# A two-layer FFN chain behind attention on one core: state products of two column pairs in one group inside a projection

## The chip, the cores and the metric

The kernel runs on 1 core of one Trainium2 chip. The metric is the device time of one execution in microseconds (us), lower is better. Engines are called TensorE (PE in the profile; PEld is its weight load), VectorE (DVE), ScalarE (ACT), GpSimd (POOL) and SyncE (SP, the DMA queue).

## The reference

x is (8 token blocks, 8 heads, 512 tokens, 64), state is (8, 8, 32, 64). For each block and head the tokens read the states with softmax attention, and the states read the tokens:

```
scores = scale * x @ state^T ; a = softmax(scores) ; xread = a @ state
scores2 = scale * state @ x^T ; a2 = softmax(scores2) ; sread = a2 @ x
rows = concat([xread, sread])          # 8 * 544 = 4352 rows of 512
y = (silu(rows @ w_gate) * (rows @ w_val)) @ w_out        # inner width 1536
h = y @ w_in2 ; out = (max(h,0) + alpha*min(h,0)) @ w_out2 # inner width 2048
```

## The kernel before

The rows of xread are never formed. Since xread = a @ state, the first FFN's gate and value for a token block are a @ (state @ w). So for each block b and each pair of 128-wide columns j (NJ1 = 6 pairs, of gate and of value together 512 columns) the kernel forms the **state products** state @ w, 128 rows (4 heads of 32 states) by 512 columns, one for each of two units g (`StateTimesW`, L566 to 592). A unit issues four products, one for each head, each a stationary tile of 64 rows by 32 columns and 512 moving columns. Unit g = 0 lies on rows 0 to 63 of the array, g = 1 on rows 64 to 127, and its four heads on the four groups of 32 columns. In float32 each is two matmul instructions, so a pair (b, j) has 16. The result stands in a PSUM bank. `hi` (L584, ScalarE, printed as the helper's L122) copies it as float32r, and `lo` (L588, VectorE, helper L128) subtracts that from it. Both parts go to an SBUF tile `sw` and are the stationary operands of gate and value.

All large products are done as three float32r passes over high and low parts (`PASSES`, L19): high by high, high by low, low by high.

`ffn1` (L702) goes through the 12 column tiles f of a block, here called **iterations**: the gate's 6 matmuls into PSUM bank `g` and Silu on ScalarE (`silu`, L648); the value's 6 into bank `v` and a multiplication on VectorE (`times`, L655); `split` into a high part (ScalarE, L663) and a low part (VectorE, L667); and the projection of the *previous* tile, 3 matmuls into each of four accumulators e = 0 to 3 (`project`, L678). In iteration 0 the projection is the last one of the block before, whose four accumulators are then copied out (`give`, L697). Between these, `fill(f, 0)` runs after the gate, `fill(f, 1)` after the split, and `fill(f, 2)` after the projection, from a table of slots. Gate(f) uses the state products of pair f // 2.

The slots of a block (`ffn1_slots`, L749) hold: the state products of pair j in slot (2j - 2, 2), that is behind the projection of iteration 2j - 2 and one iteration ahead of gate(2j); those of the next block's pair 0 in slot (10, 2); `paced` steps of the second FFN's weight preparation in iterations 1, 2, 5, 6, 9, 10 (two ScalarE, two VectorE and one GpSimd instruction, and further ones from a list, `one_later`); and the next block's attention, for its two halves of the heads g = 0 and 1 in iterations 2, 3, 5, 6, 6 and 6, 7, 9, 10, 10 (L782). Its loads stand in iterations 0 and 4 (L780). Attention's scores (L241), turned sums (L314) and state reads (L325) use TensorE for short groups, always into the two PSUM banks of the tag `aux`.

PSUM has eight banks: four accumulators, `g`, `v` and two `aux`. Before the change the state products use the two `aux` banks, one for each unit. The `sw` tiles come from 16 tiles of the tag `t4`, which the hidden tiles h, the raw x tiles and the prepared weights of the second FFN share.

The order on TensorE is the order in which the code issues (`manual_schedule` for PE, L724). The order on ScalarE, VectorE, GpSimd and SP is set by a planner that takes ready work by program order in its own model of time; each engine then works its list strictly in that order. The start (blocks 0 and 1) has an order of all engines written out by hand (L25). `ffn1` runs for blocks 2 to 7 (XT = 2, L933). Behind them come a small block of 256 state rows and the second FFN, which are not touched.

Of the kernel before, what the change touches and what calls it, by code (L numbers as in the profile page):

```python
# [70 lines left out]
def attention_and_two_ffns(ctx: ExitStack, tc: tile.TileContext, x, state, w_gate, w_val,  # L71
                           w_out1, w_in2, w_out2, alpha, out):
    nc = tc.nc
    B, H, S, D = x.shape
# [4 lines left out]
    P = 128  # L79
    T = S + Ns  # L80
    NPAIR = H // 2
    NG = H // 4
    NF1, NF2 = F1 // P, F2 // P
    NJ1, NJ2 = NF1 // 2, NF2 // 2
# [4 lines left out]
    XT = 2  # L89
# [12 lines left out]
    def name(s):  # L102
        uid[0] += 1
        return f"{s}_{uid[0]}"

    def t8(shape, dt, s):
        return p8.tile(shape, dt, tag="t8", name=name(s))

    def t4(shape, dt, s):
        return p4.tile(shape, dt, tag="t4", name=name(s))  # L110

    def t2(shape, dt, s):
        return p2.tile(shape, dt, tag="t2", name=name(s))

    def psum(shape, tag, bufs=1):
        return ps.tile(shape, F32, tag=tag, name=name(tag), bufs=bufs)

    def aux(shape):
        return psum(shape, "aux", 2)
# [28 lines left out]
    stt, xq, xn, wraw, wo1, sw, a1, srs = {}, {}, {}, {}, {}, {}, {}, []  # L148
# [49 lines left out]
    def load_xq(b, g, jj):  # L198
        t = t2([P, S // 32, 32], F32, "xq")
        for hp in range(2):  # L200
            for e in range(2):
                q = 64 * hp + 32 * e
                nc.sync.dma_start(
                    t[q:q + 32],
                    x[b, 4 * jj + 2 * hp + g].rearrange("(t i) d -> i t d", i=32)[:, :, 32 * e:32 * e + 32])
        xq[b, g, jj] = t

    def load_xn(b, g, eng=nc.sync, n=1):
        src = x[b].rearrange("(h g) (p c) d -> g p h c d", g=NG, c=SC)[g]
        t = t4([P, 4, SC, D], F32, "xn")  # L210
        for i in reversed(range(n)):
            h = slice(4 // n * i, 4 // n * (i + 1))
            eng.dma_start(t[:, h].rearrange("p h c d -> p h (c d)"), src[:, h].rearrange("p h c d -> p h (c d)"))
        xn[b, g] = t.rearrange("p h c d -> p c h d")
# [335 lines left out]
    later = []  # L550
# [7 lines left out]
    for j in range(NJ2):  # L558
        for src, take in ((words(w_in2, 0, NPAIR, 2 * P * j, 2 * P * (j + 1)), take_w2(j)),
                          (words(w_out2, 2 * j, 2 * j + 2, 0, DM), take_wo2(j))):  # L560
            n = src.shape[1] // 2
# [4 lines left out]
    class StateTimesW:  # L566
        def __init__(self, b, j, g):
            self.b, self.j, self.g = b, j, g

        def product(self):  # L570
            b, j, g = self.b, self.j, self.g
            if b >= XT:
                sw.setdefault((b, j), []).append(t4([P, 2, 4 * P], F32R, "sw"))
            elif g == 0:
                t = t8([P, NG, 2, 4 * P], F32R, "sw")
                sw[b, j] = [t[:, g] for g in range(NG)]
            self.o = aux([P, 4 * P])
            q = slice(64 * g, 64 * g + 64)
            for c in range(NPAIR):
                nc.tensor.matmul(self.o[Ns * c:Ns * (c + 1), :], stt[b][q, 2 * c + g, :],  # L580
                                 wraw[j][q, c].rearrange("p k f -> p (k f)"), start=True, stop=True)
# [9 lines left out]
            self.hi()  # L591
            self.lo()

    def state_times_w(b, j):
        sw.pop((b, j), None)
        us = [StateTimesW(b, j, g) for g in range(NG)]
        for u in us:
            u.product()
        for u in us:
            u.parts()  # L600


    class Block:


        def __init__(self, n, lhs, rhs, nk, keep=False):
            self.n, self.lhs, self.rhs, self.nk, self.keep = n, lhs, rhs, nk, keep
            self.acc, self.p, self.hid = None, {}, {}
            self.banks = lambda f: ("g", "v")

        def product(self, f, which, tag):
# [66 lines left out]
        def project(self, f):  # L678
            if f == 0:
                self.start()  # L680
            for e in range(NPAIR):
                self.project_part(f, e)
            self.hid.pop(f)

# [39 lines left out]
    with tc.manual_schedule(engines={mybir.EngineType.PE}):  # L724
# [7 lines left out]
        def load_x(b, g):  # L732
            for jj in range(2):
                load_xq(b, g, jj)
            load_xn(b, g)

        def attention(b, at, later):

            for g in range(NG):
                u = att[b, g]  # L740
                for f, stage in zip(at, [[lambda u=u: u.xt(0), lambda u=u: u.xt(1)],
                                         [u.scores, u.first_cols, u.second_max, u.first_max, u.first_sub,
                                          u.second_exp, u.first_exp],
                                         [u.first_sum, u.first_eps, u.first_over, u.first_scale, u.second_sum, u.second_turn, u.second_copy],
                                         [u.second_read, u.second_times], [u.first_parts]]):
                    for th in stage:
                        yield f + later * g, th

        def ffn1_slots(b):  # L749
            slots = {}  # L750

            def put(f, i, th):
                slots.setdefault((f, i), []).append(th)

            def paced(th=stream2.step):
                with tc.issue_after(blocks[b].gated.ins):
                    th()

            for j in range(1, NJ1):
                put(2 * j - 2, 2, lambda j=j: state_times_w(b, j))  # L760
            for f in range(NF1):
                if f in STEPS2:
                    put(f, 1, paced)
                put(f, 2, one_later)
            if b == B - 1:
                put(6, 1, load_alpha)
                put(8, 0, turn_alpha)
                gen = load_xs()
                for f in range(4, 8):
                    put(f, 0, lambda: next(gen))  # L770
                put(5, 0, first_load)
                for i in range(4):
                    put(7 + i, 2, lambda i=i: first_sub(i))
                for i in range(2):
                    put(NF1 - 3 + i, 1, lambda i=i: paced(lambda: split_w(i)))
            if b + 1 < B:
                nb = b + 1
                put(0, 0, lambda: after(lambda: load_state(nb)))
                u, v = att[nb, 0], att[nb, 1]
                for g in range(NG):  # L780
                    put(4 * g, 0, lambda g=g: load_x(nb, g))
                for f, th in attention(nb, (2, 3, 5, 6, 6), 4):  # L782
                    put(f, 0, th)
                put(NF1 - 2, 2, lambda: state_times_w(nb, 0))
            return slots

        def block(b):
# [53 lines left out]
        blocks = [block(b) for b in range(B)]  # L841
# [61 lines left out]
        with tc.manual_schedule(engines=set(ENGINES)):  # L903
            for word in START.split():
                word, _, tag = word.partition("@")
# [10 lines left out]

        todo = {}
        todo[1, 2] = [lambda: load_x(XT, 1)]
        for f, th in attention(XT, (0, 1, 4, 5, 5), 4):
            todo.setdefault((1, f), []).append(th)  # L920
        del todo[1, 0], todo[1, 1][0]
        todo.setdefault((1, 10), []).append(lambda: state_times_w(XT, 0))
        todo.setdefault((1, 8), []).append(lambda: stream2.load(2))
        for b in range(XT):
            for f in range(NF1):
# [490 lines left out]
```

## Time and profile before

| | |
|---|---|
| median of 3 runs | 1374.06 us (1374.06 to 1375.16) |
| profiled execution | 1374.58 us, span 1372.8 us |
| TensorE busy | 1352.6 us (99%) |
| VectorE busy | 1041.9 us (76%) |
| ScalarE busy | 816.3 us (59%) |
| GpSimd busy | 564.4 us (41%) |
| mean granted TensorE clock | 0.997 |

The span is the profiled time from the first to the last instruction. A busy TensorE isn't TensorE at its peak: matmuls overlap, and the time from one group's start to the next group's start says what a group costs. In a timeline each line has a start, a length and the number of instructions merged into it.

### The profile page before, as it was taken

How to read it: one execution, taken by the hardware profiler on the slowest of the kernel's cores; microseconds unless marked ns; L12 is line 12 of the kernel's file. 1: busy time of each engine (PE TensorE's matmuls, PEld its weight loads, DVE VectorE, ACT ScalarE, POOL GpSimd, SP SyncE). 2: the span in 40 equal slices, each digit the busy share in tenths (PEclk: the TensorE clock that was granted, in tenths of full speed). 3: DMA queues.
4: the chain of work that ended last, by engine and by line, in shares of the span. 5: the costliest groups of instructions: out<-in, count | busy, mean ns of one | idle time of the engine just before them, and what ended most of it. 6: DMA issues, size and time to landing. Idle time of an engine off the chain costs nothing.

```text
span 1372.8 us, 20789 instructions
## 1 busy us (share of the span) xinstructions
PE 1352.6 (99%) x7315; PEld 1067.7 (78%) x7315; DVE 1041.9 (76%) x1600; ACT 816.3 (59%) x1419; POOL 564.4 (41%) x430
## 2 busy tenths in 40 slices
PE   7999999999999999999999999999999999999997
PEld 5668777767767777777998888888888888888886
DVE  7987446777787677665757789889998889888651
ACT  7875245555555645543557677665776677666642
POOL 5642102232231223120036655666566665666611
PEclk9999999999999999999999999999999999999999
DMA  9431433766757576452517797789877987786782
GB/s 347 152 127 34 133 95 78 203 171 169 198 149 208 147 202 172 145 160 94 172 44 253 223 314 237 209 240 330 275 208 207 315 304 228 226 257 208 285 315 90
DMA packets 265057, 271.94 MB, mean 198 GB/s; under 512 B 122472, under 2 KB 189048, under 8 KB 263928
## 3 DMA queue, kind: packets, MB, share of 16 engines
q1 hardware_dynamic: 264408, 270.47, 64.0%
q8 instruction: 58, 0.95, 0.3%
q14 instruction: 47, 0.39, 0.1%
q10 hardware_dynamic: 544, 0.13, 0.0%
HBM read 206.05 MB, written 64.49 MB: 197 GB/s over the span
## 4 chain that ended last, share of the span: by engine, by line
PE 93%; DVE 3%; DMA 3%; issue 1%; ACT 1%; POOL 0%; SPq 0%; DVEq 0%; ACTq 0%; POOLq 0%
PE acc L1178 22%; PE acc L688 19%; PE v L619 10%; PE g L619 10%; PE v L1065 9%; PE g L1065 6%; PE aux L1065 6%; PE aux L580 3%; PE acc L1244 2%; PE acc L619 1%; PE aux L241 1%; PE v L1260 1%; DMA wo<-ws2d 1%; DMA ws2d<-sp 1%; PE aux L325 1%; PE g L1260 1%
## 5 line engine op out<-in xcount | busy, mean ns | idle before, releaser
L1178 PE MATMUL acc<-h,wo 128*128 128x512 f32 x1344 | 340.9, 390 | 0.7 <-DVE sum L1189 0.7
L688 PE MATMUL acc<-h,wp 128*128 128x512 f32 (+1 forms) x1296 | 295.6, 379 | 1.1 <-DVE h L128 1.1
L1178 PEld LDWEIGHTS acc<-h,wo 128*128 128x128 f32 x1344 | 251.5, 188 | 53.4 <-DVE sum L1189 0.9
L688 PEld LDWEIGHTS acc<-h,wp 128*128 128x128 f32 x1296 | 233.8, 188 | 50.2 <-issue 2.5
L1034 POOL TENSOR_TENSOR u<-u,m 128x512 f32<-128x512 f32 x96 | 128.1, 1334 | 290.6 <-ACT m L1033 253.3
L128 DVE TENSOR_TENSOR h<-u,h 128x512 fp32r<-128x512 f32 x160 | 152.2, 968 | 16.0 <-ACT h L122 15.6
L619 PE MATMUL g<-a,sw 128*128 128x512 f32 x576 | 153.9, 402 | 0.0
L122 ACT ACTIVATE h<-u 128x512 fp32r<-128x512 f32 x160 | 100.2, 630 | 89.3 <-POOL u L1077 87.7
L619 PE MATMUL v<-a,sw 128*128 128x512 f32 x576 | 150.9, 397 | 0.0
L619 PEld LDWEIGHTS g<-a,sw 128*128 128x128 f32 x576 | 105.0, 189 | 57.6 <-issue 30.2
L1065 PE MATMUL v<-x,w 128*128 128x512 f32 x576 | 146.3, 389 | 0.0
L1189 DVE TENSOR_TENSOR sum<-acc,sum 128x512 f32<-128x512 f32 x184 | 125.5, 683 | 24.7 <-PE acc L1178 24.2
L619 PEld LDWEIGHTS v<-a,sw 128*128 128x128 f32 x576 | 105.5, 188 | 31.8 <-issue 8.1
L1065 PEld LDWEIGHTS v<-x,w 128*128 128x128 f32 x576 | 107.7, 188 | 22.1
L128 DVE TENSOR_TENSOR h<-h,h 128x512 fp32r<-128x512 f32 (+1 forms) x80 | 80.2, 1004 | 40.7 <-ACT h L122 40.7
L429 POOL TENSOR_TENSOR m<-m,raw 128x512 int32<-128x512 int32 x32 | 46.4, 1449 | 156.4 <-DVE m L427 96.1
L1077 POOL TENSOR_TENSOR u<-u,u 128x512 f32<-128x512 f32 x64 | 104.3, 1630 | 5.0
L128 DVE TENSOR_TENSOR sw<-aux,sw 128x512 fp32r<-128x512 f32 x96 | 62.8, 683 | 54.1 <-ACT sw L122 53.6
L122 ACT ACTIVATE sw<-aux 128x512 fp32r<-128x512 f32 x96 | 52.7, 595 | 79.3 <-PE aux L580 73.8
L1033 ACT ACTIVATE m<-m,alpha_sb 128x512 f32<-128x512 f32 (+1 forms) x144 | 99.4, 690 | 0.0
L122 ACT ACTIVATE h<-s 128x512 fp32r<-128x512 f32 (+1 forms) x84 | 50.5, 601 | 82.0 <-DVE s L655 81.9
L1065 PE MATMUL aux<-x,w 128*128 128x512 f32 x384 | 97.6, 389 | 0.0
(159 smaller groups left out, 2144.9 us busy)
## 6 DMA issues: line engine op xcount, KB each, us to landing
wo<-ws2d SPq DMA_DIRECT2D x224, 256.0 KB, 4.9
w<-w2d SPq DMA_DIRECT2D x104, 512.0 KB, 5.3
w2d<-sp SPq DMA_DIRECT2D x32, 512.0 KB, 4.0
x2r<-x2d SPq DMA_DIRECT2D x25, 512.0 KB, 6.0
w<-w2d SPq DMA_DIRECT2D x48, 256.0 KB, 5.2
x2d<-xo SPq DMA_DIRECT2D x32, 256.0 KB, 2.8
raw<-in_moe_w_in_dram SPq DMA_DIRECT2D x16, 512.0 KB, 4.2
raw<-in_moe_w_out_dram SPq DMA_DIRECT2D x16, 512.0 KB, 4.0
```

The lines of the kernel that those rows point to most:

```text
L122: return nc.scalar.activation(o, i, AF.Copy)
L128: (eng or nc.vector).tensor_tensor(out=o, in0=src, in1=hi.bitcast(F32), op=ALU.subtract)
L429: nc.gpsimd.tensor_tensor(out=m, in0=m, in1=lo, op=ALU.add)
L580: nc.tensor.matmul(self.o[Ns * c:Ns * (c + 1), :], stt[b][q, 2 * c + g, :], wraw[j][q, c].rearrange("p k f -> p (k f)"), start=True, stop= ...
L619: nc.tensor.matmul(o[:, :self.n], self.lhs(f, k, a, which), self.rhs(k, c), start=k == 0 and i == 0, stop=k == self.nk - 1 and i == len(PA ...
L688: nc.tensor.matmul(self.acc[e][:, :self.n], wo1[f // 2][:, f % 2, a, e * P:(e + 1) * P], t[:, c, :self.n], start=(self.n == S and f == 0 a ...
L1033: nc.scalar.activation(n, n, AF.Copy, scale=alpha_sb[:, f:f + 1])
L1034: nc.gpsimd.tensor_tensor(out=out, in0=out, in1=n, op=ALU.add)
L1065: nc.tensor.matmul(o, w[:, a, q], x[k][:, q, e], start=start and n == 0, stop=stop and n == 5, skip_group_check=True)
L1077: nc.gpsimd.tensor_tensor(out=o, in0=x0, in1=x1, op=ALU.subtract)
L1178: nc.tensor.matmul(o, w[:, f, a, e], h[:, q], start=first and i == 0, stop=i == 5, skip_group_check=True)
L1189: nc.vector.tensor_tensor(out=r, in0=o, in1=r, op=ALU.add)
```

## The change

The function `state_times_w(b, j)` becomes `states_times_w(*pairs)`. It takes one or two pairs, issues the products of all their units, and then all their parts. The units' banks are, in order, `g`, `aux`, `aux`, `v`. A block gets a table `amid`: what stands in it for tile f is issued in the middle of the projection of f, behind accumulators 0 and 1. Pairs 1 and 2 stand together in the projection of tile 0 (which runs in iteration 1), pairs 3 and 4 in that of tile 4 (iteration 5), and pair 5 with the next block's pair 0 in that of tile 8 (iteration 9; in the last block pair 5 alone). The pair (2, 0), issued ahead of block 2, stays where it is, with bank `g` for its first unit. The attention's and the loads' places are now written as (iteration, slot) pairs with the same iterations and slot 0 as before.

```diff
-        def product(self):
+        def product(self, tag="aux"):
...
-            self.o = aux([P, 4 * P])
+            self.o = aux([P, 4 * P]) if tag == "aux" else psum([P, 4 * P], tag)
...
-    def state_times_w(b, j):
-        sw.pop((b, j), None)
-        us = [StateTimesW(b, j, g) for g in range(NG)]
-        for u in us:
-            u.product()
+    def states_times_w(*pairs):
+        us = [StateTimesW(b, j, g) for b, j in pairs for g in range(NG)]
+        for u, tag in zip(us, ('g', 'aux', 'aux', 'v')):
+            u.product(tag)
         for u in us:
             u.parts()
...
-            self.acc, self.p, self.hid = None, {}, {}
+            self.acc, self.p, self.hid, self.amid = None, {}, {}, {}
...
             for e in range(NPAIR):
+                if e == 2:
+                    self.amid.pop(f, lambda: None)()
                 self.project_part(f, e)
...
-        def attention(b, at, later):
+        def attention(b, at):
...
+        ATTENTION = (((2, 0), (3, 0), (5, 0), (6, 0), (6, 0)), ((6, 0), (7, 0), (9, 0), (10, 0), (10, 0)))
+        LOADS = (((0, 0), (0, 0)), ((4, 0), (4, 0)))
...
-            for j in range(1, NJ1):
-                put(2 * j - 2, 2, lambda j=j: state_times_w(b, j))
+            for j in range(1, NJ1, 2):
+                pairs = [(b, j)] + ([(b, j + 1)] if j + 1 < NJ1 else [(b + 1, 0)] if b + 1 < B else [])
+                blocks[b].amid[2 * j - 2] = lambda pairs=pairs: states_times_w(*pairs)
...
-                for g in range(NG):
-                    put(4 * g, 0, lambda g=g: load_x(nb, g))
-                for f, th in attention(nb, (2, 3, 5, 6, 6), 4):
-                    put(f, 0, th)
-                put(NF1 - 2, 2, lambda: state_times_w(nb, 0))
+                for g, (q, n) in enumerate(LOADS):
+                    put(*q, lambda g=g: [load_xq(nb, g, jj) for jj in range(2)])
+                    put(*n, lambda g=g: load_xn(nb, g))
+                for (f, i), th in attention(nb, ATTENTION):
+                    put(f, i, th)
...
-        for f, th in attention(XT, (0, 1, 4, 5, 5), 4):
+        for f, th in attention(XT, ((0, 1, 4, 5, 5), (4, 5, 8, 9, 9))):
...
-        todo.setdefault((1, 10), []).append(lambda: state_times_w(XT, 0))
+        todo.setdefault((1, 10), []).append(lambda: states_times_w((XT, 0)))
```

## Rows read from the trace of the kernel before

**Rows 1.** The page: the chain that ended last, by engine.

```profile
PE 93%; DVE 3%; DMA 3%; issue 1%; ACT 1%; POOL 0%; SPq 0%; DVEq 0%; ACTq 0%; POOLq 0%
```

**Rows 2.** Busy time of each engine from 181.84 us, and clock, DMA share, GB/s.

```profile
181.84:648.83 466.99, 464.73 (x2699) 337.64 (x2697) 334.26 (x614) 249.42 (x452) 108.68 (x94) 1.00 0.58 159
```

**Rows 3.** Waits of PE from 181.84 us on: total us, times, longest.

```profile
PE aux L241 <- DVE sw L128: 1.2, 4, 0.3
PE acc L688 <- DVE h L128: 1.1, 1, 1.1
```

**Rows 4.** Line 580 between 170 and 650 us: min/median/max ns, first and last start.

```profile
L580 PE MATMUL aux<-raw,stt x576: 589/601/613, 178.0 to 631.8; 64*32 64x512 f32 x192
```

**Rows 5.** Timeline of PE in block 4, no attention work: start us, length us.

```profile
341.41 2.88 PE L688 MATMUL acc<-h,wp 128*128 128x512 f32 x12
344.22 1.09 PE L580 MATMUL aux<-raw,stt 64*32 64x512 f32 x16
345.24 1.65 PE L619 MATMUL g<-a,sw 128*128 128x512 f32 x6
346.73 1.54 PE L619 MATMUL v<-a,sw 128*128 128x512 f32 x6
348.11 2.88 PE L688 MATMUL acc<-h,wp 128*128 128x512 f32 x12
350.83 1.52 PE L619 MATMUL g<-a,sw 128*128 128x512 f32 x6
352.19 1.52 PE L619 MATMUL v<-a,sw 128*128 128x512 f32 x6
```

**Rows 6.** Line 580 in slices of one group: window, length, PE busy (matmuls running), PEld.

```profile
318.50:318.60 0.10, 0.09 (x8) 0.09 (x16) 1.00 0.00 0
...
318.96:319.02 0.06, 0.06 (x16) 0.00 (x0) 1.00 0.00 0
```

**Rows 7.** Timeline of PE behind the group of the start.

```profile
178.97 3.03 PE L688 MATMUL acc<-h,wp 128*128 128x512 f32 x12
181.84 1.52 PE L619 MATMUL g<-a,sw 128*128 128x512 f32 x6
```

**Rows 8.** Timeline of PE around the scores of iterations 3 and 7, block 4.

```profile
357.38 1.65 PE L619 MATMUL g<-a,sw 128*128 128x512 f32 x6
358.96 1.08 PE L241 MATMUL aux<-xt,bd 128*64 128x512 f32 x4
...
384.32 1.65 PE L619 MATMUL g<-a,sw 128*128 128x512 f32 x6
386.27 1.08 PE L241 MATMUL aux<-xt,bd 128*64 128x512 f32 x4 [0.30 <-DVE sw L128]
```

**Rows 9.** Timeline of all engines around one group.

```profile
318.51 1.09 PE L580 MATMUL aux<-raw,stt 64*32 64x512 f32 x16
...
319.64 1.09 ACT L122 ACTIVATE sw<-aux 128x512 fp32r<-128x512 f32 x2 [2.07 <-PE aux L580]
320.27 0.69 DVE L128 TENSOR_TENSOR sw<-aux,sw 128x512 fp32r<-128x512 f32 x1 [1.97 <-ACT sw L122]
...
321.24 0.65 DVE L128 TENSOR_TENSOR sw<-aux,sw 128x512 fp32r<-128x512 f32 x1
```

**Rows 10.** The sw tiles, 196.7 to 650 us: what VectorE idled for (us, times).

```profile
  ACT sw L122: 46.7, 27
```

**Rows 11.** Timelines of VectorE in iteration 9 of block 3 and around a later group.

```profile
325.32 1.84 DVE L128 TENSOR_TENSOR h<-s,h 128x512 fp32r<-128x512 f32 x1
...
332.08 1.09 PE L580 MATMUL aux<-raw,stt 64*32 64x512 f32 x16
...
334.84 1.28 DVE L128 TENSOR_TENSOR sw<-aux,sw 128x512 fp32r<-128x512 f32 x2
```

**Rows 12.** Timelines of PE and VectorE in iteration 5 of block 3.

```profile
296.06 2.90 PE L688 MATMUL acc<-h,wp 128*128 128x512 f32 x12
...
297.42 0.68 DVE L655 TENSOR_TENSOR s<-s,v 128x512 f32<-128x512 f32 x1
```

More of the change, by code (lines that the diff above doesn't have):

```diff
@@ L735, in load_x @@
             load_xn(b, g)
-        def attention(b, at, later):
+        def attention(b, at):
             for g in range(NG):
                 u = att[b, g]
-                for f, stage in zip(at, [[lambda u=u: u.xt(0), lambda u=u: u.xt(1)],
+                for f, stage in zip(at[g], [[lambda u=u: u.xt(0), lambda u=u: u.xt(1)],
                                          [u.scores, u.first_cols, u.second_max, u.first_max, u.first_sub,
@@ L746, in attention @@
                     for th in stage:
-                        yield f + later * g, th
+                        yield f, th
+        ATTENTION = (((2, 0), (3, 0), (5, 0), (6, 0), (6, 0)), ((6, 0), (7, 0), (9, 0), (10, 0), (10, 0)))
+        LOADS = (((0, 0), (0, 0)), ((4, 0), (4, 0)))
         def ffn1_slots(b):
```

## The prediction

> **What bounds the kernel now.** I read the profile from the whole to the stage. The chain that ended last is 93% TensorE [rows 1], so the end is set by what TensorE does and by what makes it wait. The change touches the stage in which token blocks 2 to 7 run through the first FFN. That is 181.84 to 648.83 us, from block 2's first product to that of the small block behind block 7. There TensorE is busy for 464.73 of 466.99 us, VectorE for 334.26 (72%), ScalarE for 249.42 (53%), and the granted clock is 1.00 [rows 2], the 2.4 GHz level. So the stage is worth what its TensorE instructions last. The waits of TensorE confirm it: from there on it lost 1.2 us in four waits of the attention scores for a VectorE part of a state product, and 1.1 us in one wait for the low part of a hidden tile [rows 3]. Little else is to be won by removing waits. What can be won is time inside the TensorE stream itself, and that is where I looked next.
>
> **What a group of state products costs.** L580 issues 16 matmuls of 64x32 for a column pair (two units g, four heads each, two passes each). The timeline of a stretch without attention work shows the price. With a group: projection 341.41 to 344.22 (2.81 us), group to 345.24 (1.02), gate to 346.73 (1.49), value to 348.11 (1.38). Without: projection to 350.83 (2.72), gate to 352.19 (1.36), and value as long as gate, since both are six matmuls [rows 5]. The sum with is 6.70, without 5.44: a group costs 1.26 us. Of that only a part is streaming. In the first 0.10 us eight matmuls run, and between 318.96 and 319.02 all sixteen have begun [rows 6]: the eight tiles run side by side and the second eight follow 0.45 to 0.51 us behind the first eight. I take 0.45, the lower end, which is twice the spacing of gate's matmuls (1.36 / 6 = 0.227). Two passes stream for 0.90 us, and 1.26 - 0.90 = 0.36 us is paid for going from full-array matmuls to small tiles and back. From 178 us on there are 36 groups (x576 matmuls over 16 each) [rows 4]. The first is the pair (2, 0) ahead of the stage, which stays alone. That leaves five for each of blocks 2 to 7 and one for the next block's first pair in blocks 2 to 6: 35.
>
> **The change part by part.**
> 1. Two pairs in one group, 35 groups to 18 (three for each of six blocks; in block 7 the third holds one pair). The passes stay, 17 switches go: 17 x 0.36 = 6.1 us. If the spacing is 0.51, a switch is 1.26 - 1.02 = 0.24 and the gain 4.1. If the second pair cannot follow without a drain, the gain is 0; a loss is excluded only if the doubled group adds no wait (below). I take 6.1: the second pass of a group reuses the same tiles with new weights and follows at 0.45 [rows 6], and the second pair does the same thing once more.
> 2. The group stands inside a projection, two column groups before and two after, where it stood between projection and gate. One group of the start already lies between projections: the 12 matmuls behind it last 178.97 to 181.84, 2.87 us [rows 7], 0.15 more than 2.72. Behind a group the gate and value pay 0.13 and 0.02, also 0.15. The place costs nothing more.
> 3. The scores of iterations 3 and 7 no longer come right behind a group that holds both aux banks. In iteration 7 of block 4 the gate ahead of the scores lasts 384.32 to 386.27, 1.95 us, against 357.38 to 358.96, 1.58, in iteration 3 [rows 8]; four such [rows 3] at 0.37 make 1.5 us. By the waits view it is 1.2. In the new order the last group before these scores lies one and a half iterations back, so the aux banks are long free: -1.5.
> 4. New deadlines. Let c be the start of a doubled group. The first pair's products end at c + 1.09 (the length of a single group's records [rows 9]), the group hands over at c + 4 x 0.45 + 0.12 = c + 1.92, six projection matmuls with the exit take 1.36 + 0.13, and the gate wants its weights and bank g at c + 3.41, 2.32 us behind the first products. Before, a whole iteration lay between. What must fit: ScalarE's high part and VectorE's low part of the first unit. In the present order they end at 320.96, 1.36 us behind the products' end at 319.60 [rows 9]; 0.96 us is spare. The second unit's are needed 0.7 us and more into the gate and end 2.29 behind [rows 9]; no wait. The fourth unit holds bank v until its low part is read: three more low parts at 0.6 us each (two in a row take 1.28, one 0.69 [rows 9, 11]) end 3.2 us behind, and value begins at 2.32 + 1.36 = 3.68. Spare 0.45, and more in iterations 6 and 10, where the attention read stands ahead of value. So these hide if the two engines serve them at once. VectorE mostly did: 27 times, over the 34 groups of this view, it sat idle until ScalarE's part came [rows 10]. One foreign VectorE instruction of 0.7 us ahead would cost 0.25 us at value, in iteration 2 alone. For such cases I put 0.9 us in all (six of them at 0.15).
> 5. Two banks that were only gate's and value's now also take products. Bank g must have been read by Silu and bank v by the multiplication of the same iteration. In a late case, iteration 5 of block 3, the projection starts at 296.06 and the multiplication ends at 298.10, 2.04 us behind it [rows 12]. The fourth unit writes bank v from 1.36 + 0.09 + 0.90 = 2.35 on (half a projection, the way in, two passes). It fits by 0.3, and by more where the two low parts that VectorE now does ahead of it in these iterations are gone. Bank g is wanted 0.9 us earlier, but Silu needs no value. No cost; if the cover goes, TensorE waits for what is missing, some tenths.
> 6. Buffers: the four sw tiles of a group are taken from the 16 shared t4 tiles at once, where two were taken twice. No more than four are live either way, since the group stands behind the last use of the pair before. No cost; without a free tile ScalarE would wait for a store, and where it waits ahead of sw now it is for TensorE, as at 319.64 [rows 9].
> 7. Everything else keeps its count and place. The attention stages and loads are written as pairs with the old positions, no DMA is added or moved, and SP and POOL issue what they did. What may move is the order that the planner gives ScalarE and VectorE.
>
> **Sum.** -6.1 - 1.5 + 0.9 = -6.7. The profiled execution took 1374.58 us (a span of 1372.8 and 1.8 around it), so 1367.9; it stands 0.5 above the median of the runs, 1374.06, so 1367.4 for a median. Behind the stage TensorE is nearly without waits [rows 3], so what is saved should arrive at the end.
>
> **The rivals.**
> Evacuation binds (same). Four banks must be emptied behind one group of 1.9 us, by 4 x 0.60 of ScalarE and 4 x 0.6 of VectorE. For: VectorE is 72% busy, and from the group's start to value it also owes a multiplication, the paced weight step and a low part of the hidden tile. Against: the idle VectorE of [rows 10]. If gate or value waits 0.4 us in each of 18 groups, 7.2 of the 7.6 us go back: 1373.7. The Trainium skill, "TensorEngine Tiling (Array Packing)", section PSUM Bottleneck, says that tiling speeds TensorE but not the evacuation of PSUM, so that the copy may become the bound; by it this rival is the rule, and the trace so far does not bear it out.
>
> The queue ahead of the first low part (slower). VectorE serves in order. A hidden tile's low part once lasted 1.84 us, and once the state parts began at 334.84, 1.67 us behind products that ended at 333.17 [rows 11], where 0.67 is shown above. If the planner puts such long instructions ahead of the first unit in iterations 5 and 9, where the paced step and the attention sums fall, two of 1.84 us begun 0.6 us before the products end leave at 3.1, the first low part ends at 3.8 and the gate waits 1.5, twelve times: 18 us, so 1374.1 - 7.6 + 18 = 1384.5. It turns the sign when the mean delay at the gate passes 7.6 / 18 = 0.4 us (slower beyond 0.6), which needs a first low part 2.7 us behind its product. The one case comes to 1.67 + 0.69 = 2.4.
>
> Half the saving (still faster). The second pair drains after all, or the spacing is 0.51 and the aux banks come late: -3.1 - 1.5 + 0.9 = -3.7, 1370.4.
>
> That the change does nothing is hardly possible: TensorE's order is written out by hand, so the groups do merge.
>
> **How the numbers follow.** Forecast 0.60, half the saving 0.12, evacuation 0.16, queue 0.12. About 0.2% (2.75 us) is what a measurement can tell from no change. The first two lie below 1371.3: faster 0.72. Evacuation is within: 0.16. The queue: slower 0.12. The range runs from all of it with no new wait and the one hidden-tile wait gone too (1374.06 - 6.1 - 1.5 - 1.1 = 1365.4, rounded down for the small terms) to just above the evacuation case, 1374.2. Beyond it lie the queue case and some 0.06 on both sides.
>
> **What would show it.** Right: L580 appears as 17 groups of x32 of about 2.0 us in the timeline and one of x16, and a doubled one costs about 2.2 us over the same matmuls without it; the waits of scores for sw are gone; the stage is some 7 us shorter and the rest as long as before. Evacuation would show as TensorE waits of gate or value for sw, queue as long ones for the gate alone, with foreign VectorE work before them. The forecast is wrong if the second sixteen matmuls begin later than 0.95 us behind the first, or if waits for sw add to over 4 us.

## The result and the profile after

| | before | after |
|---|---|---|
| median beside each other, 4 runs each | 1374.61 us (1374.06 to 1375.39) | 1363.42 us (1361.52 to 1364.02) |
| profiled execution | 1374.58 us, span 1372.8 | 1363.69 us, span 1361.9 |
| stage, block 2's first gate to the small block | 466.99 us | 455.78 us |

The ratio is 0.9916, with a 95% interval of 0.9899 to 0.9933: 11.2 us faster, where 6.7 were forecast, and below the range, which began at 1365.0. (The profiled execution of one later kernel, the ninth, was disturbed and took 6.58 ms, so its trace isn't read and its median alone is told.)

All of the gain lies in the stage. In the page of the kernel after, the chain that ended last is TensorE still more than in [rows 1]:

```profile
PE 96%; DMA 2%; DVE 1%; POOL 0%; issue 0%; ACT 0%; SPq 0%; POOLq 0%; ACTq 0%
```

The stage by engine (the view of [rows 2]: window, length, then PE, PEld, DVE, ACT and POOL, clock, DMA share, GB/s), on the kernel after:

```profile
182.63:638.40 455.77, 455.77 (x2698) 342.38 (x2697) 333.18 (x614) 250.75 (x452) 109.87 (x94) 1.00 0.58 163
```

TensorE is now busy in all of it, and the clock is 1.00 as before. VectorE and ScalarE are busy for about as long as before (334.26 and 249.42 us then), so the gain lies in TensorE's stream. The waits of TensorE from the stage on, the view of [rows 3], have one line left, which lies behind the stage and is in the view of before as well (L1178 there):

```profile
PE acc L1183 <- DVE sum L1194: 0.7, 1, 0.7
```

Line 580 by its forms, the view of [rows 4], shows the new banks:

```profile
L580 PE MATMUL g<-raw,stt x152: 589/601/613, 178.7 to 625.3; 64*32 64x512 f32 x152
...
L580 PE MATMUL v<-raw,stt x136: 589/589/589, 193.1 to 601.4; 64*32 64x512 f32 x136
```

Bank v holds the fourth unit of doubled groups alone, eight matmuls each, so there are 136 / 8 = 17 of them; bank g serves these 17 and the two single groups, (2, 0) and the last (152 / 8 = 19).

The timeline of TensorE that answers to [rows 5], block 4 on the kernel after:

```profile
344.19 1.52 PE L689 MATMUL acc<-h,wp 128*128 128x512 f32 x6
345.64 0.63 PE L580 MATMUL g<-raw,stt 64*32 64x512 f32 x4
345.66 0.63 PE L580 MATMUL aux<-raw,stt 64*32 64x512 f32 x4
346.09 0.61 PE L580 MATMUL g<-raw,stt 64*32 64x512 f32 x4
...
346.55 0.61 PE L580 MATMUL v<-raw,stt 64*32 64x512 f32 x4
...
346.98 0.61 PE L580 MATMUL v<-raw,stt 64*32 64x512 f32 x4
347.51 1.65 PE L689 MATMUL acc<-h,wp 128*128 128x512 f32 x6
349.01 1.52 PE L618 MATMUL g<-a,sw 128*128 128x512 f32 x6
...
354.45 1.52 PE L618 MATMUL g<-a,sw 128*128 128x512 f32 x6
355.90 1.08 PE L241 MATMUL aux<-xt,bd 128*64 128x512 f32 x4
```

Read it by starts. The two units of a pair run side by side (345.64 and 345.66), and passes begin at 345.64, 346.09, 346.55 and 346.98, 0.45 us apart and the last 0.43. So the second pair follows without a pause. The way in costs 344.19 to 345.64 = 1.45 less the 1.36 that six matmuls last; the group lasts 1.87 to 347.51; the way out is 1.50 less 1.36. Together 0.09 + 1.87 + 0.14 = 2.10, where two single groups cost 2 x 1.26. The last two lines show a gate ahead of scores, at 1.45 us, where [rows 8] have 1.95 and 1.58.

**Where 11.2 us came from**, by summing TensorE's starts in the stage over kinds of matmul, before to after: gate 106.1 to 100.0, states 35.7 to 32.9, transposes (L314) 5.0 to 3.9, projection 201.0 to 200.0, all else together -0.3. Each time runs from a start to the next start. The gate's share is large because it held the way out of the group ahead of it, and the wait of the scores behind it. Ordered by cause, as the timelines show them:

| cause | forecast | after |
|---|---|---|
| 17 switches fewer | 17 x 0.36 = 6.1 | 17 x (2 x 1.26 - 2.10) = 7.1 |
| scores no longer wait for the aux banks | 1.5 | 4 x 0.38 = 1.5 |
| new waits | -0.9 | 0 |
| transposes no longer wait for the aux banks | not in the sum | 1.2 |
| the one wait for a hidden tile is gone | at the low end of the range only | 1.5 |
| sum | 6.7 | 11.3 |

The fourth cause is not in the view of TensorE's waits at all, since there the weight load waits and not the matmul. Timeline of TensorE on the kernel before, iteration 9 of block 3:

```profile
321.02 0.75 PE L314 MATMUL aux<-ident,e 128*128 128x128 f32 x4
321.53 1.64 PE L619 MATMUL v<-a,sw 128*128 128x512 f32 x6
```

and the waits of the weight loads there:

```profile
PEld aux L314 <- DVE sw L128: 2.8, 10, 0.3
```

On the kernel after, in block 2:

```profile
214.53 0.63 PE L314 MATMUL aux<-ident,e 128*128 128x128 f32 x4
214.92 1.64 PE L618 MATMUL v<-a,sw 128*128 128x512 f32 x6
```

Four transposes take 0.39 us from start to next start instead of 0.51. The group just ahead of them had held the aux banks until VectorE's low part. Ten such groups and those of L806 make 1.2 us.

The fifth cause is a matter of ScalarE's list. Timeline of all engines on the kernel before, block 7, iteration 6:

```profile
610.51 0.68 DVE L655 TENSOR_TENSOR s<-s,v 128x512 f32<-128x512 f32 x1
...
612.84 0.60 ACT L648 ACTIVATE s<-g 128x512 f32<-128x512 f32 x1 [4.31 <-PE g L619]
613.33 0.62 ACT L122 ACTIVATE h<-s 128x512 fp32r<-128x512 f32 x1
...
615.55 2.83 PE L688 MATMUL acc<-h,wp 128*128 128x512 f32 x11 [1.05 <-DVE h L128]
```

The multiplication ended at 611.19, so the high part of that tile could have been copied then. ScalarE was idle, but the *next* tile's Silu stood ahead of that copy on its list and waited for its gate until 612.84. The high part left 2.1 us late, the low part behind it later still, and the projection, from 614.01 to the group at 618.32, took 4.31 us where [rows 5] have 2.81: 1.5 us lost. The kernel after has no such wait in the stage.

**The deadlines** fell as item 4 worked them out. Timeline of TensorE, ScalarE and VectorE around the group at 371.25 in iteration 5 of block 4, the answer to [rows 9], on the kernel after:

```profile
371.25 0.63 PE L580 MATMUL g<-raw,stt 64*32 64x512 f32 x4
...
372.38 0.60 ACT L122 ACTIVATE sw<-g 128x512 fp32r<-128x512 f32 x1 [0.96 <-PE aux L580]
...
373.01 0.69 DVE L128 TENSOR_TENSOR sw<-g,sw 128x512 fp32r<-128x512 f32 x1 [0.59 <-ACT sw L122]
...
373.62 1.28 DVE L128 TENSOR_TENSOR sw<-aux,sw 128x512 fp32r<-128x512 f32 x2
...
374.62 1.52 PE L618 MATMUL g<-a,sw 128*128 128x512 f32 x6
374.81 0.68 DVE L128 TENSOR_TENSOR sw<-v,sw 128x512 fp32r<-128x512 f32 x1
...
376.65 0.73 PE L618 MATMUL v<-a,sw 128*128 128x512 f32 x2
```

With c = 371.25 the first low part ends at c + 2.45 and the gate starts at c + 3.37: 0.92 to spare (forecast 2.45, 3.41 and 0.96). The fourth low part ends at c + 4.24, value starts at c + 5.40 here and at c + 4.73 in iteration 2, where no state read stands ahead: 0.49 to spare (forecast 0.45). In twelve of the 17 groups the parts end within 0.01 us of this. In four, those of iteration 9 in blocks 2 to 5, VectorE puts a transposition of the state (L172, 0.43 us) behind the first low part, and the fourth ends at c + 4.57; value starts at c + 5.40 there, so it costs nothing. The least to spare is 0.43, in iteration 5 of block 7, where no state read stands ahead of value: the fourth low part ends at c + 4.30, value starts at c + 4.73.

### The profile page after: what moved, and what is told of

Its sections match the earlier page's. It is cut to its first block, busy times and chain, and to the rows that moved or that the text cites. A ratio compares the mean times of both kernels' runs of the same rounds, so it can differ in the third digit from the quotient of the medians.

```text
span 1361.9 us, 20798 instructions
## 1 busy us (share of the span) xinstructions
PE 1343.6 (99%) x7315; PEld 1072.0 (79%) x7315; DVE 1043.4 (77%) x1600; ACT 817.0 (60%) x1419; POOL 564.1 (41%) x430
## 4 chain that ended last, share of the span: by engine, by line
PE 96%; DMA 2%; DVE 1%; POOL 0%; issue 0%; ACT 0%; SPq 0%; POOLq 0%; ACTq 0%
PE acc L1183 22%; PE acc L689 21%; PE v L618 11%; PE g L618 10%; PE v L1070 9%; PE g L1070 6%; PE aux L1070 6%; PE aux L580 2%; PE acc L1249 2%; PE g L580 1%; PE acc L618 1%; PE aux L241 1%; PE v L1265 1%; DMA wo<-ws2d 1%; PE aux L325 1%; PE g L1265 1%
## 5 line engine op out<-in xcount | busy, mean ns | idle before, releaser
L689 PE MATMUL acc<-h,wp 128*128 128x512 f32 (+1 forms) x1296 | 300.1, 380 | 0.0
L618 PE MATMUL g<-a,sw 128*128 128x512 f32 x576 | 149.5, 394 | 0.5 <-POOL a L128 0.5
L429 POOL TENSOR_TENSOR m<-m,raw 128x512 int32<-128x512 int32 x32 | 49.8, 1557 | 150.0 <-ACT h L122 66.3
L647 ACT ACTIVATE s<-g 128x512 f32<-128x512 f32 (+1 forms) x78 | 45.2, 579 | 91.5 <-PE g L618 91.4
L1070 PE MATMUL g<-x,w 128*128 128x512 f32 x384 | 97.5, 389 | 0.0
```

The costliest lines, as they stand in the source:

```text
L429: nc.gpsimd.tensor_tensor(out=m, in0=m, in1=lo, op=ALU.add)
L618: nc.tensor.matmul(o[:, :self.n], self.lhs(f, k, a, which), self.rhs(k, c), start=k == 0 and i == 0, stop=k == self.nk - 1 and i == len(PA ...
L647: self.gated = nc.scalar.activation(self.p[f], self.o, AF.Silu)
L689: nc.tensor.matmul(self.acc[e][:, :self.n], wo1[f // 2][:, f % 2, a, e * P:(e + 1) * P], t[:, c, :self.n], start=(self.n == S and f == 0 a ...
L1070: nc.tensor.matmul(o, w[:, a, q], x[k][:, q, e], start=start and n == 0, stop=stop and n == 5, skip_group_check=True)
```

## The experiments

Two theories were set against each other. **Merging**: each group that goes saves its switches, wherever it stands. **Place**: most of the gain comes from leaving the spot between projection and gate, and the merging only makes that possible. Beside them stood the rivals on evacuation. All ratios are to the kernel before, run beside.

**1. Two groups, behind accumulators 0 and 1 (x1_split_pairs).** The same places and banks, but the merge undone:

```diff
...
-                if e == 2:
-                    self.amid.pop(f, lambda: None)()
+                if e in (1, 2):
+                    self.amid.pop((f, e), lambda: None)()
...
-                blocks[b].amid[2 * j - 2] = lambda pairs=pairs: states_times_w(*pairs)
+                for e, (p, tags) in enumerate(zip(pairs, (('g', 'aux'), ('aux', 'v')))):
+                    blocks[b].amid[2 * j - 2, 1 + e] = lambda p=p, tags=tags: states_times_w(p, tags=tags)
```

> The changed kernel with its doubled groups taken apart again: the first pair stands behind accumulator 0, the second behind accumulator 1 of the same projection, with the same banks and parts in the same order; only the number of switches differs, 35 instead of 18. Switch theory: by the rows of both traces two single groups cost 2 x 1.26 and a doubled one 2.10 us, so 17 x 0.42 = 7.1 us come back: 1370.5 where the changed kernel has 1363.4. Place theory (the gain comes from where the groups stand and from their banks, merging is worth little): 1363.4 to 1365.

Measured: 1377.86 us, ratio 1.0021 (1.0013 to 1.0030), the stage 469.20. That is 13.4 us over the kernel after, twice what 17 switches cost. TensorE's waits in the stage tell why:

```profile
PE acc L689 <- DVE h L128: 3.0, 2, 1.5
PE acc L689 <- ACT h L122: 1.0, 2, 0.5
```

In iteration 5 of blocks 4 and 6 the hidden tile's parts came late; with what followed them 6.6 us were lost (worked out below, from run 10). Run 1 didn't decide, since it changed ScalarE's order as well as the groups.

**2. Each pair alone inside a projection (x2_singles_inside).** Pairs stand in the projections of tiles 0, 2, 4, 6, 8 and 10, in the two aux banks:

```diff
-        for u, tag in zip(us, ('g', 'aux', 'aux', 'v')):
+        for u, tag in zip(us, ('aux', 'aux')):
...
-            for j in range(1, NJ1, 2):
-                pairs = [(b, j)] + ([(b, j + 1)] if j + 1 < NJ1 else [(b + 1, 0)] if b + 1 < B else [])
-                blocks[b].amid[2 * j - 2] = lambda pairs=pairs: states_times_w(*pairs)
+            for j in range(1, NJ1 + 1):
+                pair = (b, j) if j < NJ1 else (b + 1, 0)
+                if pair[0] < B:
+                    blocks[b].amid[2 * j - 2] = lambda pair=pair: states_times_w(pair)
```

> No merging: each pair's products stand alone inside the projection of tile 2j - 2, both units in the aux banks as before the change, gate's and value's banks left alone. Switch theory: 35 switches as before the change, but scores and transposes no longer come behind a group that holds the aux banks, so of the 11.2 us the merging's 7.1 are lost and some 3.7 stay (scores 1.5, transposes 1.2, hidden-tile wait 1.1): 1370.5 to 1371. Place theory: all of it stays, 1363.4 to 1365.

Measured: 1401.91 us, ratio 1.0189 (1.0173 to 1.0206): a miss by 31 us. The groups in iterations 3 and 7 meet the scores, which hold the aux banks until ScalarE's exponentials. Waits of TensorE, and the timeline of one such group:

```profile
PE aux L580 <- ACT e L304: 6.9, 10, 1.3
```

```profile
204.65 1.06 PE L580 MATMUL aux<-raw,stt 64*32 64x512 f32 x8
...
205.97 1.06 PE L580 MATMUL aux<-raw,stt 64*32 64x512 f32 x8 [0.27 <-ACT e L304]
```

The two units get their banks at different times, so they no longer run side by side and the group takes more than twice as long (2.32 us, 204.65 to 206.97). Some stretches of the stage ran at a clock of 0.50 on top (236 to 239 us is one), and the two stalls of run 1 are in this run too (4.0 us of waits). One part of the place theory did show: the transposes take 0.39 us as soon as no group stands ahead of them, merged or not.

**3. The same with banks g and v (x7_singles_gate_value).** The tags become `('g', 'v')`.

> Single groups inside the projection as in the second run, but in the banks of gate and value, so that scores and groups of iterations 3 and 7 no longer share the aux banks. Collision theory: the 22 us of waits of state products for an aux bank go, and what stays over the changed kernel is the 7.3 of the switches plus waits of gate in iterations 4 and 8, where VectorE is busy with the attention maxima (some 3 us in the second run): 1371 to 1375. If something else than the bank made singles inside slow: near 1400.

Measured: 1399.28 us, ratio 1.0174 (1.0160 to 1.0188): missed again. The states fell from 54.6 to 40.5 us, so the aux banks were indeed what run 2 waited for, but then the gate of iterations 4 and 8 waits for its weights. Timelines of ScalarE and TensorE behind the group at 204.57:

```profile
206.79 0.59 ACT L122 ACTIVATE sw<-g 128x512 fp32r<-128x512 f32 x1
...
208.34 1.67 PE L618 MATMUL g<-a,sw 128*128 128x512 f32 x6 [1.10 <-DVE sw L128]
```

ScalarE is busy with the exponentials there (a table load from 203.77 on, then L304 and L260 until 206.37, then a hidden tile's copy), the first copy leaves 2.2 us behind the group's start instead of 1.1, and the gate waits 1.10. Ten gates wait 12.3 us in all. That is not the whole miss: the two stalls of run 1 stand here too (3.1 us of waits, with a clock of 0.5 behind them), and the 17 switches. So iterations 3 and 7 have no room for a group inside a projection as ScalarE's list stands. Three groups in iterations 1, 5 and 9 avoid them; that needs two pairs in each.

**4. A later place, behind accumulator 2 (x3_behind_third).** `if e == 2` becomes `if e == 3`: three matmuls less between group and gate.

> The doubled group stands behind accumulator 2 instead of 1, so only 3 projection matmuls (0.68 us) cover it. In the changed kernel the first low part ends 2.45 us behind the group's start and the fourth 4.24. Deadline theory: gate is now wanted at 1.88 + 0.13 + 0.68 = 2.69, so no wait there; value at 4.05 in iteration 2, so up to 0.2 us in six groups: 1363.4 to 1364.8. If evacuation is slower when it stands closer to the next Silu and multiplication: a wait of 0.3 or more in all 18, 1369 or more.

Measured: 1368.32 us, ratio 0.9952 (0.9939 to 0.9964), the stage 5.1 us over the kernel after. The gate came at c + 2.68, behind the first low part at 2.45, without a wait, as expected. Value in iteration 2 should come at c + 4.05, but the fourth low part ends at 4.24: it starts at 4.30 in seven groups (the weight loads wait, not the matmuls, and the timeline shows one of them):

```profile
PEld v L618 <- DVE sw L128: 3.6, 7, 0.6
```

```profile
269.26 0.63 PE L580 MATMUL g<-raw,stt 64*32 64x512 f32 x4
...
271.95 1.53 PE L618 MATMUL g<-a,sw 128*128 128x512 f32 x6
273.56 1.66 PE L618 MATMUL v<-a,sw 128*128 128x512 f32 x6
```

Those are iteration 2 of six blocks and iteration 6 of block 7, and each costs 0.4. The single last group's gate waits 0.58, and three hidden tiles cost 0.5 each. The deadlines hold, but the price was put too low, and the time is 3.5 us above the expected range.

**5. Behind the whole projection (x4_behind_projection).** The call moves behind the loop over e, so that the gate follows the doubled group at once.

> The doubled group stands behind all four accumulators, directly ahead of the gate. Deadline theory: the gate is wanted 1.88 us behind the group's start and bank g is free at 2.45 plus about 0.05, a wait of 0.6 in 18 groups; value is wanted at 4.0 and the fourth low part ends at 4.24, another 0.3 in six: 10.8 + 1.8 = 12.6, so 1376, slower than the kernel before. If the place inside the projection does not matter: 1363.4 to 1365.

Measured: 1380.54 us, ratio 1.0040 (1.0028 to 1.0053), the stage 16.9 us over the kernel after. Every group now waits for the first low part, 2.50 us from the group's start to the gate's instead of 1.88:

```profile
PE g L618 <- DVE sw L128: 11.0, 18, 1.5
```

That is 0.62 us in each, as expected. The time is still 4.5 us above the 1376 expected, because value is late in seven groups, the last group's gate waits 1.5 and three hidden tiles cost 0.5 each. So a doubled group directly ahead of the gate is slower than the kernel before: evacuation is hidden only by the six matmuls ahead of the gate. (The old places stood one iteration earlier, ahead of a gate that doesn't read these products. A doubled group there was not tried; its bank g would have to be read just as soon.)

**6. Only the aux banks (x5_aux_banks_only).** All four units take `aux`, so that the second pair waits until the first is read.

> The doubled group at the changed kernel's place, but all four units in the two aux banks. Bank theory: the third unit waits for the first one's low part (2.45 us behind the group's start, wanted at 0.87) and the fourth for the second's (3.05), and the two no longer run side by side: about 2.2 us in each of 17 groups, 37 us, 1400. If the banks of gate and value do not matter: 1363.4.

Measured: 1417.69 us, ratio 1.0309 (1.0279 to 1.0339). TensorE's timeline of one group:

```profile
192.03 1.09 PE L580 MATMUL aux<-raw,stt 64*32 64x512 f32 x16
194.53 1.66 PE L580 MATMUL aux<-raw,stt 64*32 64x512 f32 x16 [1.42 <-DVE sw L128]
196.12 1.66 PE L689 MATMUL acc<-h,wp 128*128 128x512 f32 x6
```

A group takes 4.09 us instead of 1.88, which makes 37.6 for 17 as expected. The profiled execution, the shortest of four at 1411.86 us, is 48.2 over the kernel after; the other 11 us are mostly the stalls in iteration 5 as in run 1 and stretches at a clock of 0.50. Without the banks of gate and value the merge costs more than it saves.

**7. Two groups, behind accumulators 1 and 2 (x6_split_later).** Run 1 with `e in (2, 3)`: the merge undone again.

> The doubled groups taken apart once more, now behind accumulators 1 and 2. Switch theory: in the stage, states, their entries and exits take 17 x 0.43 = 7.3 us more than in the changed kernel (states 17 x 0.21, projection 17 x 0.22), as in the split before; with the planner's order undisturbed 1370.7. If hidden-tile waits as in the first split (6 us in iteration 5 of blocks 4 and 6) belong to splitting itself, 1377 again; if they are the planner's order, which any shift can change, they are elsewhere or gone while the 7.3 stay.

Measured: 1370.14 us, ratio 0.9964 (0.9952 to 0.9977): a hit. No TensorE wait for a hidden tile, and the stage is 6.88 us over the kernel after. Taken iteration by iteration, from gate start to gate start, each of the 17 that hold two groups lasts 0.38 us longer, together 6.5; the other 0.4 is value late for its last low part in seven of them, as in run 4. With the merge undone and the place kept, 4.3 of the 11.2 us stay.

**8. An earlier place, behind accumulator 0 (x8_behind_first).** `if e == 1`. More cover than in the kernel after, so by the deadlines the time should be the same.

> The doubled group stands behind accumulator 0, with 0.68 us more cover than in the changed kernel. Deadline theory: there is nothing left to hide, 1363.4 within 0.7. If the cover was still what bounds it, faster than 1362; if bank v is not yet read by the multiplication when the fourth unit comes, slower.

Measured: 1370.40 us, ratio 0.9963 (0.9949 to 0.9977): a miss by 7 us, with the two stalls of run 1 in the same places. ScalarE's and TensorE's timelines in iteration 5 of block 4:

```profile
368.34 0.60 ACT L647 ACTIVATE s<-g 128x512 f32<-128x512 f32 x1 [4.01 <-PE g L618]
...
369.94 0.61 ACT L122 ACTIVATE h<-s 128x512 fp32r<-128x512 f32 x1
...
372.62 0.77 PE L689 MATMUL acc<-h,wp 128*128 128x512 f32 x2 [1.52 <-DVE h L128]
```

The tile's multiplication had ended at 365.3. From then until 368.34 ScalarE was idle with the high part ready, which stood behind the next tile's Silu and two instructions of the paced step (L419, L420), and so left at 369.94. That is the kernel before's single case, but with more in the queue. In the kernel after, at the same place, the copy is ahead:

```profile
365.20 0.63 ACT L122 ACTIVATE h<-s 128x512 fp32r<-128x512 f32 x1 [1.03 <-DVE s L654]
...
368.19 0.60 ACT L647 ACTIVATE s<-g 128x512 f32<-128x512 f32 x1 [1.32 <-PE g L618]
```

**9 to 12. ScalarE's order pinned.** If the order is the cause of those stalls, then an edge (an added dependency) that keeps each Silu behind the high part of the tile before must remove them, and the bare effects of merge and place remain. The same edge was put into four kernels: run 8, run 1, the kernel before and the kernel after.

```diff
-            self.gated = nc.scalar.activation(self.p[f], self.o, AF.Silu)
+            with ExitStack() as behind:
+                if hasattr(self, "high") and self.n == S and not self.keep:
+                    behind.enter_context(tc.issue_after(self.high.ins))
+                self.gated = nc.scalar.activation(self.p[f], self.o, AF.Silu)
...
-            acopy(t[:, 0, :self.n], self.p[f])
+            self.high = acopy(t[:, 0, :self.n], self.p[f])
```

> The run with the group behind accumulator 0, with one edge more: from block 2 on each Silu is kept behind the high part of the hidden tile before it on ScalarE's list. Order theory: the 7 us of that run over the changed kernel come from two places (iteration 5 of blocks 4 and 6) where Silu and two weight steps stand ahead of a high part that was ready, the TensorE stall of 2.9 us there and the granted clock of 0.5 behind it; with the edge 1363.4. If the place itself (bank v not read yet) costs it: 1370 again.

> The first split (behind accumulators 0 and 1), with the same edge. Switch and order theory: only the 7.3 us of the 17 switches stay, 1370.5. If the stalls belong to splitting: 1377.9 again.

> The kernel before with the same edge. Order theory: its one wait of 1.1 us for a hidden tile's low part goes, 1373.5 where the kernel before has 1374.6, and nothing else moves. If that wait has another cause: no change.

> The changed kernel with the same edge, as a control: it shows no TensorE wait for a hidden tile, so 1363.4 within 0.7. If the edge itself delays Silu and with it the value's multiplication, 1364.5 or more, and the same must be taken off the three others.

| kernel | without edge | with edge | ratio with edge (95%) | stage with edge |
|---|---|---|---|---|
| behind accumulator 0 | 1370.40 | 1363.88 | 0.9914 (0.9901 to 0.9928) | not read |
| two groups, accumulators 0 and 1 | 1377.86 | 1369.57 | 0.9959 (0.9947 to 0.9972) | 462.57 |
| before | 1375.27 | 1373.64 | 0.9986 (0.9977 to 0.9994) | 466.01 |
| after | 1363.42 | 1362.72 | 0.9909 (0.9894 to 0.9925) | 455.78 |

The medians of the first column were taken beside a kernel before of 1374.6 to 1375.5, those of the second beside one of 1375.27, so the last tenths of a difference between the columns mean nothing. Run 8 comes back to the 1363.4 that its deadlines gave, run 1 to 1369.57 where its switches gave 1370.5. The control, the kernel after with the edge, can't be told from the kernel after without it; its stage is the same. The kernel before gains 1.6 us by the medians and 1.0 in the stage: the wait in its block 7 goes (1.5), and a wait of 0.5 behind another group comes.

With the order the same in both, two groups instead of one cost 462.57 - 455.78 = 6.79 us in the stage. TensorE's timeline of the two groups with the edge (run 10), iteration 1 of block 2:

```profile
190.29 0.84 PE L692 MATMUL acc<-h,wp 128*128 128x512 f32 x3
191.06 0.63 PE L580 MATMUL g<-raw,stt 64*32 64x512 f32 x4
...
192.08 0.96 PE L692 MATMUL acc<-h,wp 128*128 128x512 f32 x3
192.97 0.63 PE L580 MATMUL aux<-raw,stt 64*32 64x512 f32 x4
...
193.99 1.66 PE L692 MATMUL acc<-h,wp 128*128 128x512 f32 x6
195.48 1.53 PE L618 MATMUL g<-a,sw 128*128 128x512 f32 x6
```

From 190.29 to 195.48 are 5.19 us, and the twelve projection matmuls without a group last 2.72: two groups cost 2.47, where the doubled one costs 2.10. All 17 such iterations are 0.38 longer than in the kernel after, from gate start to gate start, which makes 6.5. The rest of the 6.79 is no switch: in iteration 8 of blocks 4 and 6 a weight load of the projection waits for its hidden tile's low part (0.5 together; run 8, which merges, lost as much there), and the last, single group is 0.2 cheaper.

So the 11.2 us are 6.5 for the merge, 1.5 of scores, 1.2 of transposes and 1.5 of the hidden tile. Some 0.7 more is the place: two single groups between projection and gate cost 2 x 1.26 = 2.52, inside a projection 2.47, 17 times. About 0.2 goes back at the last group, whose gate waits. Scores and transposes are costs of holding the aux banks ahead of attention work; they are read from the timelines, not from a run of their own. The hidden tile is the planner's order, which the change turned by chance and not by its design: the edge alone frees the kernel before of it.

## Why the prediction was right and wrong

**The mechanism held.** TensorE sets the stage's end, and the gain is time inside its stream. The second pair began 0.91 us behind the first (0.95 was the forecast's own limit) and no wait for sw came, so "half the saving" is ruled out. Item 3 (-1.5) and items 5 and 6 (no cost) came out as put. What failed is the size: the forecast fell 4.5 us short, by the steps below.

**Items 1 and 2, the size of a switch, were too low**: 0.36 us forecast and 0.38 measured at the same place (runs 7 and 10), 6.5 us instead of 6.1; and the place, put at nothing, gave the 0.04 more that make 0.42 against the old spots, 7.1 in all. The ways in and out came as in [rows 5], but for the 0.02 at value, which is gone; the doubled group lasted 1.87, not the 1.92 of item 4, because its last passes follow at 0.43, not 0.45, and its end is shorter. So it cost 2.10 and not 2.16, 17 times: 1.0 us.

**Item 4, an allowance of 0.9 for new waits, was too high**: there are none. The deadlines were right to 0.05 us each, so there was nothing left for the allowance to stand on: I had worked out 0.45 to spare (the item's own terms, 3.68 less 3.2, give 0.48) and then paid for six foreign VectorE instructions that no row showed. One did come, in four groups (L172), but in iteration 9, where the state read ahead of value covers it.

**Item 7 failed**, by 2.7 of the 4.5 us, and with it the range. "Everything else keeps its count and place" was true, but it gave no term to what the old group had held up. Two things followed from views that I had: the weight loads of the transposes stood right behind groups in the aux banks, just as the scores did, and I priced the scores alone because [rows 3] showed matmuls' waits and not weight loads' (1.2 us). The hidden tile's wait of 1.1 in [rows 3] I put at the range's low end; it went, and with its restart it was worth 1.5. That part was luck: the sum had no reason for it, and runs 1 and 8 got longer waits of the same kind out of a slightly different place. Without an allowance, and with these two, the sum would have been -6.1 - 1.5 - 1.2 - 1.5 = -10.3, and 1363.8.

**Evacuation.** The trace before spoke against this rival, and at this place it does not bind: all four low parts end at least 0.43 us before value wants them. With three matmuls less behind the group value is late by 0.25 (run 4), with six less the gate by 0.62 (run 5), and beside the exponentials by 1.10 (run 3). The rule of the Trainium skill, "TensorEngine Tiling (Array Packing)", section PSUM Bottleneck, is thus borne out in these three runs and not in the change itself.

**The queue** turned out to be a real danger, but on another engine and for another tile: not long VectorE work ahead of a state part, but ScalarE's Silu ahead of a hidden tile's high part. By the profiled executions, of which run 8's was the longest of five, it cost 6.6 us in run 1 and 8.2 in run 8, the lower clock behind the stalls included; by the medians the edge gave back 8.3 and 6.5. The change was free of it; I had no way to see that from the trace before, where [rows 3] had a single case, and I named this only as an order that "may move".

## What to carry to other kernels

Where TensorE is the bound, count the changes between array tilings and merge groups: one group of small tiles less gave back 0.38 us here, and a merge pays if the evacuation of all its banks fits under the matmuls that follow, which can be worked out to 0.05 us from the durations of copy and low part in the trace. Look also at the waits of weight loads behind a group, and at what else wants its banks. Before two variants are compared, pin the order of a ready instruction against one that waits for TensorE: a planner's turn there moved times by 6.5 to 8.3 us, as much as the effect in question.

## What was not expected of the hardware

The granted clock fell behind some short stalls of TensorE. In run 8, around the stall at 370.60, windows of the trace (columns as in [rows 2]) show:

```profile
370.60:373.30 2.70, 1.17 (x3) 0.48 (x3) 2.67 (x5) 1.51 (x3) 1.16 (x1) 0.98 0.01 3
373.30:375.00 1.70, 1.70 (x17) 0.45 (x24) 1.70 (x3) 0.00 (x0) 0.43 (x1) 0.50 0.21 14
```

TensorE was busy for 1.17 of 2.70 us, then the clock stood at 0.50, the 1.2 GHz level, and the doubled group that followed took 3.46 us (373.32 to 376.78) instead of 1.88. Set against the same stretch of the kernel after, and allowing for the three matmuls that stand behind the group here and ahead of it there, the group began 2.6 us late and lasted 1.6 longer, so a stall of 2.6 us cost 4.2. In block 6 the same came to 3.1 and 1.0. The Trainium skill, "TensorE: Matmul & The Clock Gate", section "HAM oscillation — how this bites in real kernels", says that idle stretches between bursts of matmuls set the clock back to half; this trace agrees, with 0.50 behind that stretch, though the waits that the section describes are longer than the 0.49 and 1.52 us here. Nor did every such stall do it. Around the kernel before's wait of 1.05 us the clock stayed at 1.00, and run 1 has the same two waits in block 4 (0.49 and 1.53 us, up to 375.89) with the full clock behind them:

```profile
375.90:377.60 1.70, 1.70 (x19) 0.49 (x19) 1.70 (x2) 0.00 (x0) 1.09 (x1) 1.00 0.01 5
```

In block 6 of run 1 the clock did fall (0.61 from 534.91 to 536.55). What decides between the two stays open here; the price of a stall can't be read from its length alone.
